# A Fourier-mixing and squared-RELU kernel: 89 instead of 82 halved steps, folds and transform placed earlier, the row read on ScalarE's queue

## The chip, the cores and the metric

The kernel runs on one core of a Trainium2 chip. The metric is the device time of one execution in microseconds. Three executions of the kernel before the change gave 614.35, 612.79 and 614.75 us, with a median of 614.35 us. Below, PE is TensorE, ACT is ScalarE, DVE is VectorE, POOL is GpSimd and SP is SyncE.

## The reference

The input x has shape 8 x 3008 x 256. The real part of its two-dimensional Fourier transform (over the sequence and over the 256 features) is taken as 24064 tokens of 256 features, and goes through a feed-forward layer with a squared RELU.

```python
X = np.fft.fft(x, axis=1)
X = np.fft.fft(X, axis=2)
attn = X.real.astype(np.float32).reshape(8 * 3008, 256)

h = np.maximum(attn @ w_in, 0.0)          # w_in: 256 x 2048
out = (h * h @ w_out).astype(np.float32)  # w_out: 2048 x 256
```

## The kernel before

**Symmetry.** The transform of real data is symmetric, so the kernel works with 12040 *columns* (8 batches, with 4 x 376 + 1 each) that stand for a frequency and its mirror. For each it computes two rows of 128: zc (the cosine part over the features) and zs (the sine part). The feature transform is folded into the first weights. gh holds three forms of them: gh[:, 0] for zc, gh[:, 1] for zs, and gh[:, 2], which is -2 times gh[:, 1] but for the first row, which is zero (the scale is made in `turn2`). With p = gh0 zc and q = gh1 zs, the hidden value of a column is p + q and that of its mirror is p - q, but for row 0 of zs (the d = 128 feature), which enters both with the same sign.

**Windows.** The columns are cut into 25 windows, here called blocks 0 to 24: the first six are 240, 512, 376, 376, 512 and 448 wide, the others 512 and the last 360. The loop `for w in range(NW)` goes over them.

**Steps.** A block has NST = 8 steps s, one for each pair of 128 rows of the 2048 hidden ones. Between the matmuls of a step, `others(s)` issues all other work, in this order: the jobs of at[s], a share of the second layer (`ffn2_steps`, L620) of the block before, post[s], and a share of the transform of the units that begin in the next block (`z_steps`, L482). The order on every queue is the order in which the code issues the instructions.

A *plain* step (`pq`, `turn`, `square`) runs four matmuls for p + q (L731, L732), ScalarE's RELU (L741), then, after `others`, two more matmuls that turn the sum in PSUM into p - q (L737), and a second RELU. The square of each half is made by VectorE (L746), or for the first half by ScalarE (L744) if the step stands in `by_act`.

A *halved* step (`half_q`, `half_p`, `row_sum`, `halves`) runs two matmuls for q (L756), which ScalarE copies out times -2 into sn (L764), and after `others` two more that add p to q in PSUM (L770), which ScalarE copies into hd (L772). VectorE does the rest for a group of one to three neighbouring steps: two rows per step, eb times wv, put back what the sign change took from row 0 (L780); sn becomes sn + rows (L784); the mirror's value is hd + sn (L795); a maximum with 0 (L796); and the square into h2 (L797). L795 to L797 are issued by `halves` in the step after the group's last.

PLAN says which steps of a block are halved and in what groups, and which squares of plain steps ScalarE makes. `plan(w)` picks one of three; blocks 0, 1, 2 and 4 have none. The h2 of a block is read in the next block: step 0 there multiplies the first 128 columns with all 16 chunks of h2, chunks 0 to 7 first, then 8 to 15. Columns of the mirrored half come from step 4 on.

**The row.** Row 0 of zs is needed on all partitions as eb. `row_spread(w)` writes it to DRAM (zr, L581, ScalarE's queue), and reads it back spread over 128 partitions (eb, L583, SP's queue, which also carries the stores of out, L600).

**Folds.** Each batch is folded before its transform, on VectorE, by `fold_jobs(i)`: even fold of the features (L352 to L354), its cosine sum (L362), odd fold (L357, which also issues the load of the next x on POOL), sine sum (L365), differences (L372), a small column (L377 to L379), even sums (L383, written to DRAM on POOL), and their read back. The first two are the *first folds* of a batch; `first_at` places them in steps 0 and 5 of a block. `fold_at` places the rest, two blocks ahead of the batch's columns, at steps 0 and 4 to 7. `late_at` places the four late folds (L408, L419) at steps 3 to 6.

**The transform.** A unit is a batch's odd or even frequencies (16 units). Its plus part is copied by ScalarE into the zc and zs of the windows it falls into (L491); its mirrored columns come from VectorE (L498, `minus`). `lo` and `hi` say over which steps a block spreads it, from lo to hi - 1.

```python
lo, hi = 0, NST - 1
...
if s >= lo:
    for j in spread(zl, s - lo, hi - lo) if s < hi else []:
        j()
```

Of the buffers, PSUM has two for a step's sums, hd has two, sn has two, h2 has two.

By these rules blocks 10, 13, 16 and 19 have fold work and a transform, 11, 14, 17 and 20 have five halved steps and a transform, and 12, 15 and 18 have late folds and the next batch's first folds.

Of the kernel before, what the change touches and what calls it, by code (L numbers as in the profile page):

```python
# [12 lines left out]
ALU = mybir.AluOpType  # L13

HS = 32.0
P = 128
# [12 lines left out]
def kernel(  # L29
# [14 lines left out]
    nc = tc.nc  # L44
# [12 lines left out]
    FIRST = [240, 512, 376, 376, 512, 448]  # L57
    R23 = float(2.0 ** 23)

    PLAN = {0: (((1, 2), (3, 4), (5,)), (0, 6, 7)), 1: (((1, 2), (3, 4)), (0, 5, 6)), 2: (((1, 2), (3,)), (0, 5, 6))}  # L60

    RQ = (1, 3, 5, 0, 2, 4)

# [12 lines left out]
    g = 0  # L76
# [4 lines left out]
    NW = len(wins)  # L81
# [9 lines left out]
    g = 0  # L91
# [91 lines left out]
    def small(shape, name):  # L183
        return const.tile(shape, F32, name=name)
# [271 lines left out]
    def zwin(w):  # L456
        if w not in zc:
            zc[w] = zp.tile([P, WN], F16, name="zc", tag="zc")
            zs[w] = zp.tile([P, WN], F16, name="zs", tag="zs")
        return zc[w], zs[w]  # L460
# [67 lines left out]
    def run(*jobs):  # L528
        for j in jobs:
            j()  # L530
# [34 lines left out]
    wv = small([P, NFC], "wv")  # L565
# [6 lines left out]
        nc.vector.tensor_scalar(out=wv, in0=pv[:, 0:NFC], scalar1=2.0, scalar2=None, op0=ALU.mult)  # L572

    eb = {}

    def row_spread(w):

        wn = wins[w][1]
        t = eb[w] = tmp.tile([P, WN], F16, name="eb", tag="kf")
        zr = drp.tile([1, WN], F16, name="zr", tag="zr")  # L580
        nc.scalar.dma_start(out=zr[0:1, 0:wn], in_=zwin(w)[1][0:1, 0:wn])  # L581
        src = zr[0:1, 0:wn]
        nc.sync.dma_start(out=t[:, 0:wn], in_=bass.AP(tensor=src.tensor, offset=src.offset, ap=[[0, P], [1, wn]]))  # L583

    def store(osb, p0, g0, m, minus, eng=nc.sync):

# [71 lines left out]
    fold_at, late_at = {}, {}  # L658
# [3 lines left out]
    NST = NFC // 2  # L662

    first_at = {}
    for w, i in fold_at.items():
        first_at[w - 1] = i

    def plan(w):

        if w < 3 or w == 4:  # L670
            return (), ()
        return PLAN[min(2, 2 * (w in fold_at) + (w in first_at) + (w in late_at))]

    def halved(w):

        return plan(w)[0]
# [4 lines left out]
    for w in range(NW):  # L681
        g0, wn = wins[w]
        h2 = h2p.tile([P, NFC, 2 * WN], F16, name="h2", tag="h2")
        zcw, zsw = zwin(w)

        lo, hi = 0, NST - 1
        at = [[] for _ in range(NST)]
        post = [[] for _ in range(NST)]
        if w == 0:
# [1 line left out]
        elif w == 1:  # L691
# [3 lines left out]
            lo, hi = 6, 7  # L695
# [11 lines left out]
        elif w == win_of(col_of[1, 1]) - 1:  # L707
            for st in range(4):
                at[st] = folds[1]["late"][st : st + 1]
            lo = 4  # L710
# [16 lines left out]
        def pq(s):  # L727
            ph = phs[s] = ps_h.tile([P, 2, 512], F32, name="ph", tag="psh")
            for a in range(2):
                f0 = (2 * s + a) * P  # L730
                nc.tensor.matmul(ph[:, a, 0:wn], gh[:, 0, f0 : f0 + P], zcw[:, 0:wn], start=True, stop=False)  # L731
                nc.tensor.matmul(ph[:, a, 0:wn], gh[:, 1, f0 : f0 + P], zsw[:, 0:wn], start=False, stop=True)  # L732

        def turn(s):
            for a in range(2):
                f0 = (2 * s + a) * P
                nc.tensor.matmul(phs[s][:, a, 0:wn], gh[:, 2, f0 : f0 + P], zsw[:, 0:wn], start=False, stop=True, skip_group_check=True)  # L737

        def square(s, sg):
            h1 = h1p.tile([P, 2, 512], F16, name="h1", tag="h1")  # L740
            nc.scalar.activation(h1[:, :, 0:wn], phs[s][:, :, 0:wn], AF.Relu)  # L741
            hv = rev_dim(h1[:, :, 0:wn], 2) if sg else h1[:, :, 0:wn]
            if sg == 0 and s in by_act:
                nc.scalar.activation(h2[:, 2 * s : 2 * s + 2, 0:wn], hv, AF.Square)  # L744
                return []
            return [lambda: nc.vector.tensor_tensor(h2[:, 2 * s : 2 * s + 2, sg * wn : (sg + 1) * wn], hv, hv, op=ALU.mult)]  # L746

        two = {s: g for g in halved(w) for s in g}
        by_act = plan(w)[1]
        sns, hds = {}, {}  # L750

        def half_q(s):
            ph = phs[s] = ps_h.tile([P, 2, 512], F32, name="ph", tag="psh")
            for a in range(2):
                f0 = (2 * s + a) * P
                nc.tensor.matmul(ph[:, a, 0:wn], gh[:, 1, f0 : f0 + P], zsw[:, 0:wn], start=True, stop=True)  # L756
            g = two[s]
            if s == g[0]:
                i = ROT[0] % 2
                ROT[0] += 1  # L760
                sns[g] = const.tile([P, 2 * len(g), WN], F16, name=f"sn{i}", tag=f"w16_{i}")
                hds[g] = tmp.tile([P, 2 * len(g), 2 * WN], F16, name="hd", tag="tt")
            i = 2 * g.index(s)
            nc.scalar.activation(sns[g][:, i : i + 2, 0:wn], ph[:, :, 0:wn], AF.Copy, bias=0.0, scale=-2.0)  # L764

        def half_p(s):
            ph, g = phs[s], two[s]
            for a in range(2):
                f0 = (2 * s + a) * P
                nc.tensor.matmul(ph[:, a, 0:wn], gh[:, 0, f0 : f0 + P], zcw[:, 0:wn], start=False, stop=True, skip_group_check=True)  # L770
            i = 2 * g.index(s)
            nc.scalar.activation(hds[g][:, i : i + 2, 0:wn], ph[:, :, 0:wn], AF.Copy, bias=0.0, scale=1.0)  # L772

        def row_sum(s):

            g = two[s]
            sn, hd = sns[g][:, :, 0:wn], hds[g][:, :, wn : 2 * wn]

            def row(a):
                nc.vector.tensor_scalar(out=hd[:, 2 * g.index(s) + a, :], in0=eb[w][:, 0:wn], scalar1=wv[:, 2 * s + a : 2 * s + a + 1], scalar2=None, op0=ALU.mult)  # L780

            jobs = [lambda: row(0), lambda: row(1)]
            if s == g[-1]:
                jobs.append(lambda: nc.vector.tensor_tensor(sn, sn, hd, op=ALU.add))  # L784
            return jobs

        def halves(s):

            if s not in two or s != two[s][-1]:
                return []  # L790
            g = two[s]
            sn, hd = sns[g], hds[g]
            hv = hd[:, :, 0 : 2 * wn]
            return [
                lambda: nc.vector.tensor_tensor(rev_dim(hd[:, :, wn : 2 * wn], 2), hd[:, :, 0:wn], sn[:, :, 0:wn], op=ALU.add),  # L795
                lambda: nc.vector.tensor_scalar(out=hv, in0=hv, scalar1=0.0, scalar2=None, op0=ALU.max),  # L796
                lambda: nc.vector.tensor_tensor(h2[:, 2 * g[0] : 2 * g[-1] + 2, 0 : 2 * wn], hv, hv, op=ALU.mult),  # L797
            ]

        def others(s):  # L800
            for j in at[s]:
                j()
            for j in spread(f2, s, NST):
                j()
            for j in post[s]:
                j()
            if s == lo:
                zl[:] = [j for zu, part, h in zj for j in zu(part, h)]
            if s >= lo:
                for j in spread(zl, s - lo, hi - lo) if s < hi else []:  # L810
                    j()
# [3 lines left out]
        for s0 in range(0, NST, ng):  # L815
            ss = range(s0, s0 + ng)
            left = halves(s0 - 1)
            if s0 in two:
                half_q(s0)
                rows = row_sum(s0)  # L820
                run(*(left[0:1] + rows[0:1] + left[1:2] + rows[1:2] + left[2:3] + rows[2:3]))
                others(s0)
                half_p(s0)
                continue
            for s in ss:
                pq(s)
            for s in ss:
                run(*(left[0:2] + square(s, 0) + left[2:3]))
            others(s0)
            for s in ss:  # L830
                turn(s)
            for s in ss:
                run(*square(s, 1))
            if s0 == hi - 1 and ng == 1 and w + 1 < NW and halved(w + 1):
                row_spread(w + 1)
            for s in ss[1:]:
                others(s)
            if s0 < hi <= s0 + ng - 1 and w + 1 < NW and halved(w + 1):
                row_spread(w + 1)
        old = (w, h2)  # L840
    for j in ffn2_steps(*old, tail=True):
        j()
# [30 lines left out]
```

## Time and profile before

| | |
|---|---|
| median of three runs | 614.35 us |
| the profiled execution | 614.29 us |
| its span in the profile | 612.4 us |
| granted TensorE clock | 0.995 |
| PE busy | 586.7 us, 4400 matmuls |
| PE weight loads busy | 423.4 us |
| ACT busy | 518.0 us |
| DVE busy | 486.7 us |
| POOL busy | 83.3 us |
| DMA | 50.20 MB |

All times within the profile count from the start of the span. A line of a timeline gives the start and the length of an instruction in us, the engine, the line of the code, the operation, what it writes and reads with the shapes, and in brackets how long the engine stood idle before it and what ended that. On PE and on VectorE instructions overlap a little, so that the time from one start to the next says more about what one costs than its own length does.

The blocks can be found in the trace by PE's first-layer matmuls. Block 12 begins at 287.57, block 13 at 311.03, block 14 at 335.64, block 15 at 359.72 and block 16 at 383.18 us. From block 11 to block 20 the pattern repeats every three blocks, some 72.15 us.

### The profile page before, as it was taken

How to read it: one execution, taken by the hardware profiler on the slowest of the kernel's cores; microseconds unless marked ns; L12 is line 12 of the kernel's file. 1: busy time of each engine (PE TensorE's matmuls, PEld its weight loads, DVE VectorE, ACT ScalarE, POOL GpSimd, SP SyncE). 2: the span in 40 equal slices, each digit the busy share in tenths (PEclk: the TensorE clock that was granted, in tenths of full speed). 3: DMA queues.
4: the chain of work that ended last, by engine and by line, in shares of the span. 5: the costliest groups of instructions: out<-in, count | busy, mean ns of one | idle time of the engine just before them, and what ended most of it. 6: DMA issues, size and time to landing. Idle time of an engine off the chain costs nothing.

```text
span 612.4 us, 11453 instructions
## 1 busy us (share of the span) xinstructions
PE 586.7 (96%) x4400; PEld 423.4 (69%) x4400; DVE 486.7 (79%) x742; ACT 518.0 (85%) x673; POOL 83.3 (14%) x125
## 2 busy tenths in 40 slices
PE   5799998999899999999999999999999999998996
PEld 2456876777677777777777767777677777776686
DVE  7787669776978978869979699778997697796980
ACT  7687788888889889889899898898988998988872
POOL 5324110012001021020022200411010200100000
PEclk9899999999999999999999999999999999999999
DMA  8927120173113531632145311543111411111112
GB/s 143 200 80 144 57 81 27 53 155 105 43 52 73 133 115 47 142 115 58 39 100 130 91 55 42 110 121 84 50 36 61 122 44 52 48 50 47 50 56 67
DMA packets 39591, 50.20 MB, mean 82 GB/s; under 512 B 4572, under 2 KB 33393, under 8 KB 39537
## 3 DMA queue, kind: packets, MB, share of 16 engines
q0 software_dynamic: 9344, 22.14, 17.9%
q1 hardware_dynamic: 29923, 27.11, 15.0%
q8 instruction: 34, 0.56, 0.4%
q10 hardware_dynamic: 270, 0.23, 0.1%
q14 instruction: 20, 0.16, 0.1%
HBM read 36.29 MB, written 27.86 MB: 105 GB/s over the span
## 4 chain that ended last, share of the span: by engine, by line
PE 63%; DVE 16%; ACT 8%; issue 6%; DMA 5%; POOL 1%; SPq 0%; ACTq 0%; DVEq 0%; POOLq 0%
PE po L620 37%; PE ph L737 5%; PE ph L770 5%; PE ph L731 4%; PE ph L732 4%; PE ph L756 4%; ACT h L741 4%; DVE h L797 3%; DVE hd L795 3%; DVE hd L796 3%; DMA out_dram<-osb 3%; PE pz L482 3%; ACT hd L772 2%; DMA w<-in_moe_w_in_dram 1%; DVE sn L784 1%
## 5 line engine op out<-in xcount | busy, mean ns | idle before, releaser
L620 PE MATMUL po<-wout,h 128*128 128x256 f16 (+1 forms) x3024 | 362.5, 273 | 1.1 <-DVE h L797 1.0
L620 PEld LDWEIGHTS <-h 128*128 128x128 f16 (+1 forms) x3024 | 296.3, 98 | 73.5 <-DVE h L797 2.5
L741 ACT ACTIVATE h<-ph 128x1024 f16<-128x1024 f32 (+4 forms) x236 | 217.3, 962 | 31.2 <-PE ph L737 16.7
L746 DVE TENSOR_TENSOR h<-h 128x1024 f16<-128x1024 f16 (+4 forms) x173 | 108.0, 641 | 52.0 <-ACT h L741 49.8
L772 ACT ACTIVATE hd<-ph 128x1024 f16<-128x1024 f32 (+3 forms) x82 | 81.4, 993 | 19.2 <-PE ph L770 17.4
L797 DVE TENSOR_TENSOR h<-hd 128x4096 f16<-128x4096 f16 (+7 forms) x50 | 91.7, 1835 | 0.4
L731 PE MATMUL ph<-zc,gh 128*128 128x512 f16 (+4 forms) x236 | 85.2, 363 | 3.8 <-DVE zc L498 3.0
L732 PE MATMUL ph<-zs,gh 128*128 128x512 f16 (+4 forms) x236 | 85.1, 363 | 0.4 <-ACT zs L491 0.4
L764 ACT ACTIVATE sn<-ph 128x1024 f16<-128x1024 f32 (+3 forms) x82 | 81.2, 990 | 0.0
L784 DVE TENSOR_TENSOR sn<-sn,hd 128x2048 f16<-128x2048 f16 (+7 forms) x50 | 49.9, 997 | 31.3 <-ACT sn L764 30.0
L737 PE MATMUL ph<-zs,gh 128*128 128x512 f16 (+4 forms) x236 | 65.5, 363 | 5.1 <-ACT h L741 3.6
L635 ACT ACTIVATE osb<-po 128x512 f32<-128x512 f32 (+3 forms) x95 | 54.6, 578 | 17.1 <-PE po L620 15.1
L744 ACT ACTIVATE h<-h 128x1024 f16<-128x1024 f16 (+3 forms) x63 | 64.8, 1029 | 2.0
L795 DVE TENSOR_TENSOR hd<-hd,sn 128x2048 f16<-128x2048 f16 (+7 forms) x50 | 49.9, 998 | 14.3 <-ACT hd L772 12.1
L780 DVE TENSOR_SCALAR hd<-eb,wv 128x512 f16<-128x512 f16 (+3 forms) x164 | 51.5, 352 | 5.8 <-DMA eb<-zr 5.8
L796 DVE TENSOR_SCALAR hd<-hd 128x4096 f16<-128x4096 f16 (+7 forms) x50 | 49.9, 997 | 0.7
L770 PE MATMUL ph<-zc,gh 128*128 128x512 f16 (+3 forms) x164 | 47.3, 370 | 1.0 <-ACT sn L764 0.8
L756 PE MATMUL ph<-zs,gh 128*128 128x512 f16 (+3 forms) x164 | 47.4, 370 | 0.0
L731 PEld LDWEIGHTS <-gh 128*128 128x128 f16 x236 | 23.0, 97 | 27.5 <-DVE zc L498 3.8
L732 PEld LDWEIGHTS <-gh 128*128 128x128 f16 x236 | 23.0, 98 | 25.1 <-issue 2.0
L425 POOL COPY xt<-xt 128x2 f16<-128x2 f16 x16 | 7.0, 469 | 206.7 <-DVE xt L408 206.7
L737 PEld LDWEIGHTS <-gh 128*128 128x128 f16 x236 | 22.3, 97 | 12.9 <-issue 8.2
(121 smaller groups left out, 381.1 us busy)
## 6 DMA issues: line engine op xcount, KB each, us to landing
out_dram<-osb SPq DMA_DIRECT2D x77, 128.0 KB
xo<-in_x_dram POOLq DMA_DIRECT2D x7, 768.0 KB
scr<-ev POOLq DMA_DIRECT2D x8, 390.0 KB, 3.3
eb<-zr SPq DMA_DIRECT2D x18, 128.0 KB
rb<-scr POOLq DMA_DIRECT2D x16, 130.0 KB
out_dram<-osb SPq DMA_DIRECT2D x12, 94.0 KB
w<-in_moe_w_in_dram POOLq DMA_DIRECT2D x2, 512.0 KB
wout<-in_moe_w_out_dram POOLq DMA_DIRECT2D x1, 1024.0 KB
```

The source lines that it names most:

```text
L620: nc.tensor.matmul(po[0:m, j * D : (j + 1) * D], h2[:, fc, q : q + m], wout16[:, fc, :], start=(fc == 0), stop=(fc == NFC - 1))
L731: nc.tensor.matmul(ph[:, a, 0:wn], gh[:, 0, f0 : f0 + P], zcw[:, 0:wn], start=True, stop=False)
L732: nc.tensor.matmul(ph[:, a, 0:wn], gh[:, 1, f0 : f0 + P], zsw[:, 0:wn], start=False, stop=True)
L737: nc.tensor.matmul(phs[s][:, a, 0:wn], gh[:, 2, f0 : f0 + P], zsw[:, 0:wn], start=False, stop=True, skip_group_check=True)
L741: nc.scalar.activation(h1[:, :, 0:wn], phs[s][:, :, 0:wn], AF.Relu)
L746: return [lambda: nc.vector.tensor_tensor(h2[:, 2 * s : 2 * s + 2, sg * wn : (sg + 1) * wn], hv, hv, op=ALU.mult)]
L756: nc.tensor.matmul(ph[:, a, 0:wn], gh[:, 1, f0 : f0 + P], zsw[:, 0:wn], start=True, stop=True)
L764: nc.scalar.activation(sns[g][:, i : i + 2, 0:wn], ph[:, :, 0:wn], AF.Copy, bias=0.0, scale=-2.0)
L770: nc.tensor.matmul(ph[:, a, 0:wn], gh[:, 0, f0 : f0 + P], zcw[:, 0:wn], start=False, stop=True, skip_group_check=True)
L772: nc.scalar.activation(hds[g][:, i : i + 2, 0:wn], ph[:, :, 0:wn], AF.Copy, bias=0.0, scale=1.0)
L795: lambda: nc.vector.tensor_tensor(rev_dim(hd[:, :, wn : 2 * wn], 2), hd[:, :, 0:wn], sn[:, :, 0:wn], op=ALU.add),
L797: lambda: nc.vector.tensor_tensor(h2[:, 2 * g[0] : 2 * g[-1] + 2, 0 : 2 * wn], hv, hv, op=ALU.mult),
```

## The change

The plan gets new groups. A block with five halved steps keeps (1,2), (3,4), (5). Blocks with fold work or late folds get four halved steps in the groups (1,2) and (4,5), with ScalarE squaring in steps 0, 3 and 6 (before they had three, (1,2) and (3), with squares in 0, 5 and 6; blocks 6 and 21 had four, (1,2) and (3,4)). Block 7 goes from four, (1,2) and (3,4), to five. Blocks 3, 5 and 9 get (1,2) and (4). So there are 89 halved steps in place of 82: block 3 has two fewer, blocks 7, 8, 10, 12, 13, 15, 16, 18 and 19 have one more.

The first folds of batches 5, 6 and 7 move from blocks 12, 15 and 18 to 11, 14 and 17. In block 3 and from block 5 on, the transform is spread over steps 0 to 5 instead of 0 to 6, and the row's write (zr) comes at the end of step 5 instead of 6. The read back (eb) goes out on ScalarE's queue after the block's last step. The rows of a group are all made at its last step instead of two in each.

```diff
-    PLAN = {0: (((1, 2), (3, 4), (5,)), (0, 6, 7)), 1: (((1, 2), (3, 4)), (0, 5, 6)), 2: (((1, 2), (3,)), (0, 5, 6))}
+    PLAN = {
+        "5": (((1, 2), (3, 4), (5,)), (0, 6, 7)),
+        "4": (((1, 2), (4, 5)), (0, 3, 6)),
+        "3": (((1, 2), (4,)), (0, 5, 6)),
+    }
...
-        nc.sync.dma_start(out=t[:, 0:wn], in_=bass.AP(tensor=src.tensor, offset=src.offset, ap=[[0, P], [1, wn]]))
+        row_back.append(lambda: nc.scalar.dma_start(out=t[:, 0:wn], in_=bass.AP(tensor=src.tensor, offset=src.offset, ap=[[0, P], [1, wn]])))
...
     for w, i in fold_at.items():
-        first_at[w - 1] = i
+        free = [v for v in range(w - 1, 6, -1) if v not in late_at and all(not v <= u < w for u in fold_at)]
+        first_at[free[0] if free else w - 1] = i
...
-        return PLAN[min(2, 2 * (w in fold_at) + (w in first_at) + (w in late_at))]
+        if w < 6 or w in first_at and w in late_at:
+            return PLAN["3"]
+        return PLAN["4" if w in fold_at or w in late_at else "5"]
...
-        lo, hi = 0, NST - 1
+        lo, hi = 0, NST - 2 if w == 3 or w > 4 else NST - 1
...
             def row(a):
-                nc.vector.tensor_scalar(out=hd[:, 2 * g.index(s) + a, :], in0=eb[w][:, 0:wn], scalar1=wv[:, 2 * s + a : 2 * s + a + 1], scalar2=None, op0=ALU.mult)
-
-            jobs = [lambda: row(0), lambda: row(1)]
-            if s == g[-1]:
-                jobs.append(lambda: nc.vector.tensor_tensor(sn, sn, hd, op=ALU.add))
-            return jobs
+                nc.vector.tensor_scalar(out=hd[:, a, :], in0=eb[w][:, 0:wn], scalar1=wv[:, 2 * g[0] + a : 2 * g[0] + a + 1], scalar2=None, op0=ALU.mult)
+
+            if s < g[-1]:
+                return []
+            return [lambda a=a: row(a) for a in range(2 * len(g))] + [lambda: nc.vector.tensor_tensor(sn, sn, hd, op=ALU.add)]
...
                 rows = row_sum(s0)
-                run(*(left[0:1] + rows[0:1] + left[1:2] + rows[1:2] + left[2:3] + rows[2:3]))
+                run(*(left[0:1] + rows[0:1] + left[1:2] + rows[1:-1] + left[2:3] + rows[-1:]))
                 others(s0)
                 half_p(s0)
+                if s0 == hi - 1 and w + 1 < NW and halved(w + 1):
+                    row_spread(w + 1)
                 continue
...
+        while row_back:
+            row_back.pop()()
         old = (w, h2)
```

More of the change, by code (lines that the diff above doesn't have):

```diff
@@ L574 @@
     eb = {}
+    row_back = []
     def row_spread(w):
```

## The prediction

> **What bounds the kernel now.** A *block* is one of the 25 windows of columns (at most 512 wide), a *step* one of its eight pairs of 128 rows of the hidden layer. I read the page's busy times first, then the busy time by block over one period of three, then VectorE's timeline in such a block, then the waits.
>
> ```profile
> PE 586.7 (96%) x4400; PEld 423.4 (69%) x4400; DVE 486.7 (79%) x742; ACT 518.0 (85%) x673; POOL 83.3 (14%) x125
> ```
>
> ```profile
> 311.03:335.64 24.61, 24.50 (x193) 17.98 (x192) 20.44 (x28) 22.46 (x30) 5.29 (x6) 1.00 0.55 117
> 335.64:359.72 24.08, 24.08 (x179) 17.41 (x178) 17.81 (x26) 21.36 (x29) 3.13 (x4) 1.00 0.29 88
> 359.72:383.18 23.46, 23.39 (x171) 16.54 (x170) 22.10 (x35) 20.87 (x25) 1.48 (x4) 1.00 0.16 49
> ```
>
> The lines are blocks 13 (with a fold), 14 (five halved steps) and 15 (late fold): length, then busy PE, PEld, DVE, ACT. PE is full in each, and within a block a 512-column matmul follows the last after 0.216 us and a 256-column one after 0.109 us. PE's work decides while nobody makes it wait. But VectorE has 22.10 of 23.46 us in block 15, and what counts for it is when its last result of a block arrives:
>
> ```profile
> 345.95 1.23 DVE L795 TENSOR_TENSOR hd<-hd,sn 128x2048 f16<-128x2048 f16 x1 [0.67 <-ACT hd L772]
> 347.09 0.35 DVE L780 TENSOR_SCALAR hd<-eb,wv 128x512 f16<-128x512 f16 x1
> 347.36 1.22 DVE L796 TENSOR_SCALAR hd<-hd 128x4096 f16<-128x4096 f16 x1
> ...
> 348.75 2.29 DVE L797 TENSOR_TENSOR h<-hd 128x4096 f16<-128x4096 f16 x1
> 350.95 0.61 DVE L780 TENSOR_SCALAR hd<-eb,wv 128x512 f16<-128x512 f16 x2
> 351.67 1.23 DVE L784 TENSOR_TENSOR sn<-sn,hd 128x2048 f16<-128x2048 f16 x1
> 353.00 1.23 DVE L795 TENSOR_TENSOR hd<-hd,sn 128x2048 f16<-128x2048 f16 x1
> ...
> 360.58 1.23 DVE L797 TENSOR_TENSOR h<-hd 128x2048 f16<-128x2048 f16 x1
> 361.72 0.60 DVE L498 SCALAR_TENSOR_TENSOR zc<-es,pz 128x195 f16<-128x195 f32 x2
> ```
>
> ```profile
> 361.86 0.55 PEld L620 LDWEIGHTS <-h 128*128 128x128 f16 x6 [0.30 <-DVE h L797]
> ```
>
> From 345.95, when ScalarE has copied step 2's sums (L772), VectorE has no gap until 361.81, 15.85 us: a **tail** that is its own bound. Its last halved result (step 5) ends 2.09 us after block 15 began at 359.72. The second product of that block reads it 1.95 us in (0.87 for step 0's first four matmuls, eight of 0.109, two more), and so the weight load waits 0.30 and PE loses 0.19. VectorE idles before the tail, in steps 1 and 2, where the results that it needs don't exist yet. So each us that the change puts into the tail of block 14 is a us of PE.
>
> Block 13's tail is also gapless, from 321.04:
>
> ```profile
> 334.21 0.54 DVE L498 SCALAR_TENSOR_TENSOR zc<-es,pz 128x376 f16<-128x376 f32 x1
> 334.67 1.29 DVE L746 TENSOR_TENSOR h<-h 128x1024 f16<-128x1024 f16 x2
> ```
>
> Its last urgent result is the second of these squares (step 7), done at 335.96, 0.32 after block 14's start; PE needs it 2.39 us in (0.87 and fourteen of 0.109). Here 2.1 us are free.
>
> ```profile
> PE ph L737 <- ACT h L741: 3.6, 6, 1.4
> PE ph L731 <- DVE zc L498: 3.0, 2, 1.7
> ```
>
> These waits (total, times, longest) are the transform's: at the ends of blocks 3, 6 and 22 PE or ScalarE waits for the mirrored half (L498) queued behind VectorE's tail. Spacing of PE's matmuls beyond their streaming shows 1.9, 1.4 and 2.9 us there.
>
> **The change, part by part.** Durations are of the profiled execution, 614.29 us (span 612.4); the median is 614.35, so the sum carries over unchanged. "Slot" is start to next start.
>
> *Halved steps.* Each saves two of six first-layer matmuls, 2 x 0.216 = 0.43 us. By the plan there are 82 before and 89 after: one more in blocks 7, 8, 10, 12, 13, 15, 16, 18, 19, two fewer in block 3 (376 columns, 4 x 0.157 = 0.63). PE alone: -9 x 0.43 + 0.63 = -3.2 us. ScalarE evicts twice either way. VectorE pays: slots are 0.27 a row, 1.14 the sum, 1.14 + 1.13 + 2.20 difference, maximum and square for a pair, so 3.3 per halved step against 0.6 or 1.2 for a plain one's squares.
>
> *Rows together at a group's last step.* The rows that stood between difference, maximum and square no longer do. A row starts 0.09 before the end of what precedes it, a dependent operation 0.03 to 0.10 after it (351.67 + 1.23 to 353.00), so each uncovered dependency costs 0.12 to 0.19; I take 0.13, 0.26 a pair. The Trainium skill ("VectorE: DVE Perf Modes", the section on the DRAIN that can't be avoided) says that the next operation doesn't start until the pipe is empty and that chaining without semaphores gains nothing; by it this term would be 0 and the sum about 2 us lower, but the trace's row at 347.09 starts before 347.18 and disagrees.
>
> *Block 14's kind (11, 14, 17), first folds a block sooner.* Ahead of the step-5 square come: the fold's cosine sum at step 5 (slot 0.88, from the equal fold sum at 329.91), the zc mirror (0.52, now 361.72 to 362.24 behind the square, a step sooner ahead of it), 0.26 of uncovered dependencies, and 0.13 since the transform's twelve 0.157 us matmuls lie in six steps instead of seven and step 3 begins later. Together 1.79; nothing leaves this tail. +1.79 x 3 = +5.4. The first even fold (2.0) falls at step 0 into VectorE's idle time. It needs x a block sooner: in block 13 the last gather of x goes out on POOL at 325.68 and such a gather lands in 8.1 us (median), near 334, while VectorE gets to the fold near 339; without that cover the fold and all behind it on VectorE would wait.
>
> *Block 13's kind (10, 13, 16, 19), groups (1,2),(4,5).* Out of the tail go two rows 0.53, step 3's sum 0.60, its triple 2.48, three plain squares 1.8, together 5.4; in come four rows and a dependency 1.19, a sum 1.14, a triple 4.73, a square 0.60, dependencies 0.26, together 7.9. The end moves from 335.96 to 338.5, the next block from 335.64 to 334.93 (0.43, and a 0.28 wait for ScalarE behind two SQUAREs in a row, now apart). 3.6 after its start against 2.39: a stall of 1.3. Net -0.43 - 0.28 + 1.3 = +0.6, x 4 = +2.4.
>
> *Block 15's kind (12, 15, 18), first fold gone.* The tail is 15.7 us from 9.5 us into a block of 22.7 (3 x 2.62 and the rest at 3.05 before): it ends 2.5 late against 2.39, stall 0.2; a 0.22 wait for ScalarE goes. Net -0.45 x 3 = -1.35.
>
> *Single blocks.* 7: one step, one group and 1.2 of mirrors more before the last square (ends 194.6, block 8 from 190.0): -0.43 - 0.31 + 2.6 = +1.9. 8: a fold block without transform, -0.43 + 0.8 = +0.4. 20: like 14 without the cosine sum, +0.9. 23: +0.2. 9, 21: none. 3: +0.63 - 1.9 = -1.3. 6: -1.4 + 0.5 = -0.9. 22: -2.9 + 1.3 = -1.6, for a step sooner the mirrors come before the last triple.
>
> *The row's read on ScalarE.* The eb issue takes 0.35 on SP (L583). At the block's end it stands ahead of the next block's first RELU, 18 times, 6.3 us of ScalarE in all. Its write zr is two steps old by then; at 356.89 it was issued and at 358.01 the read went out, so 1.1 us, and ScalarE won't wait. I take 0, because PE stalls for VectorE at most of these joints while ScalarE, at 89 to 91% of a block, catches up; without this cover it is 0 to 0.35 each, up to +6.3. On SP the stores get free of the wait for zr, which costs nobody now: ScalarE's copies into osb wait for PE alone. VectorE waits for eb three times, 5.8 us in all, in idle time: 0, at most -1.
>
> Sum: 5.4 + 2.4 - 1.35 + 1.9 + 0.4 + 0.9 + 0.2 - 1.3 - 0.9 - 1.6 = **+6.0**, so 620.3 us.
>
> **Rivals.** *VectorE's tail has room (faster).* If the tail's last square comes less than 1.95 us into the next block, PE's streaming decides: -3.2, and the gaps go (1.9, 1.4, 2.9, four of 0.28, four of 0.22: -8.2), so 603. For it: VectorE is busy 79% overall. Against: that share holds the idle steps 1 and 2; the tail shows no gap, and the work is inserted into it. 0.13.
>
> *The stalls are half as long (same).* A tail 0.8 us shorter per block over some ten blocks is -8 at most; at -6 nothing is left, about 614. My tails are good to some 0.3 us. 0.12.
>
> *ScalarE takes the bound (slower still).* With 85% it is the busiest after PE, and every step costs it two evictions as before; then only its new 6.3 us show: 620.6 with no other effect, 626 on top of the sum. Against: its waits are short and on PE. The Trainium skill ("Perfetto Trace Analysis", on identifying the most-contended engine) judges TensorE by weight-load share, not by matmul share; by it, with 69%, ScalarE would be the engine to watch. The spacing of 0.216 and 0.109 us in the trace speaks against it. 0.10.
>
> The forecast has 0.65. A difference below 0.3% (1.8 us) can't be told from none. Faster: the first rival and a sliver, 0.14; same 0.12; slower 0.74. The range takes in the second rival and most of the third, 612 to 625.
>
> **What would show it.** After: PE waiting for L797's successor at the starts of blocks 12, 15, 18 some 2 us, at those of 11, 14, 17, 20 some 1.3 us; no gap at the ends of 3, 6 and 22; blocks 14 and 13 with their following stall near 25.9 and 25.2 us, 15 near 23. VectorE's tail gapless and 17.6 us in block 14. It is wrong if VectorE shows gaps in that tail, or if PE waits for ScalarE's first RELU instead.

## The result and the profile after

Four executions of the changed kernel took 621.57 us in the median (619.85 to 623.12), against 614.55 for four of the kernel before on the same chip: the ratio is 1.0118, with a 95% interval of 1.0084 to 1.0152. So the change makes the kernel 7.0 us slower; the forecast was 620.3. In the traces PE's first block begins at 21.3 to 24.7 us, whatever the kernel, and this alone shifts single runs by up to 3 us, so the text also counts from there to the end of the span: 588.95 us before and 596.33 after, 7.4 more.

The busy line of the page after:

```profile
PE 584.0 (94%) x4386; PEld 421.0 (68%) x4386; DVE 503.7 (81%) x742; ACT 519.1 (84%) x673; POOL 85.3 (14%) x125
```

PE has less work (584.0 us against 586.7), as 89 halved steps want it, and VectorE has 17.0 us more. Yet PE's share of the span fell. Where its time went shows in the busy times by block; the columns are as before, and the lines are blocks 13, 14 and 15 of the changed kernel:

```profile
312.11:336.33 24.22, 24.18 (x191) 17.78 (x190) 21.12 (x28) 22.12 (x30) 4.44 (x6) 1.00 0.57 115
336.33:361.61 25.28, 24.26 (x180) 17.33 (x179) 22.50 (x32) 21.94 (x29) 3.69 (x5) 1.00 0.28 85
361.61:386.46 24.85, 23.01 (x169) 16.34 (x168) 21.02 (x29) 20.84 (x25) 0.42 (x2) 1.00 0.16 48
```

Before, PE was busy for all but 0 to 0.11 us of each. Now blocks 14 and 15 hold 1.02 and 1.84 us in which it is idle, and together the three are 74.35 us long in place of 72.15. VectorE's timeline of block 14:

```profile
347.99 1.23 DVE L802 TENSOR_TENSOR hd<-hd,sn 128x2048 f16<-128x2048 f16 x1 [0.67 <-ACT hd L780]
349.25 1.23 DVE L803 TENSOR_SCALAR hd<-hd 128x4096 f16<-128x4096 f16 x1
350.51 2.29 DVE L804 TENSOR_TENSOR h<-hd 128x4096 f16<-128x4096 f16 x1
352.72 1.14 DVE L788 TENSOR_SCALAR hd<-eb,wv 128x512 f16<-128x512 f16 x4
353.96 1.23 DVE L792 TENSOR_TENSOR sn<-sn,hd 128x2048 f16<-128x2048 f16 x1
355.11 0.61 DVE L502 SCALAR_TENSOR_TENSOR zs<-es,pz 128x195 f16<-128x195 f32 x2
...
361.22 0.97 DVE L366 TENSOR_TENSOR ab<-fe 128x1560 f16<-128x1560 f16 x1
362.11 0.61 DVE L502 SCALAR_TENSOR_TENSOR zc<-es,pz 128x195 f16<-128x195 f32 x2
...
364.08 1.22 DVE L804 TENSOR_TENSOR h<-hd 128x2048 f16<-128x2048 f16 x1
```

The tail runs without a gap from 347.99 to 365.30, 17.31 us; it was 15.85, and 17.6 was forecast. The cosine sum (L366) and the zc mirror (L502) stand ahead of the last triple, where the forecast put them. Block 15 began at 361.61, so its last square is 3.69 us late. PE's weight loads at the start of blocks 14 and 15:

```profile
339.90 0.11 PEld L625 LDWEIGHTS <-h 128*128 128x128 f16 x2 [1.29 <-DVE h L754]
...
365.35 0.55 PEld L625 LDWEIGHTS <-h 128*128 128x128 f16 x6 [1.91 <-DVE h L804]
```

The first waits for the plain square of block 13's step 7 (L754), the second for the last halved square of block 14 (L804; this wait was 0.30 us before the change). In the waits of the whole changed kernel (total, times, longest), these two head those of PE's weight loads:

```profile
PEld L625 <- DVE h L804: 11.7, 7, 2.3
ACT h L749 <- DVE h L754: 11.8, 12, 1.9
PEld L625 <- DVE h L754: 6.5, 6, 1.3
PE ph L778 <- ACT sn L772: 2.0, 8, 0.4
```

The second and the last were not in the forecast, and come up again below.

### The profile page after: what moved, and what is told of

Read it like the earlier page. It is cut to its first block, busy times and chain, and to the rows that moved or that the text cites. A ratio compares the mean times of both kernels' runs of the same rounds, so it can differ in the third digit from the quotient of the medians.

```text
span 618.1 us, 11384 instructions
## 1 busy us (share of the span) xinstructions
PE 584.0 (94%) x4386; PEld 421.0 (68%) x4386; DVE 503.7 (81%) x742; ACT 519.1 (84%) x673; POOL 85.3 (14%) x125
## 4 chain that ended last, share of the span: by engine, by line
PE 45%; DVE 29%; issue 10%; ACT 10%; DMA 4%; POOL 1%; ACTq 0%; DVEq 0%; SPq 0%; POOLq 0%
PE po L625 27%; DVE h L804 7%; DVE hd L803 5%; DVE hd L802 5%; ACT h L749 4%; PE ph L745 4%; PE ph L778 3%; PE ph L764 3%; PE ph L739 3%; PE ph L740 3%; DMA out_dram<-osb 3%; DVE hd L788 2%; DVE h L754 2%; ACT sn L772 2%; DVE sn L792 2%
## 5 line engine op out<-in xcount | busy, mean ns | idle before, releaser
L749 ACT ACTIVATE h<-ph 128x1024 f16<-128x1024 f32 (+4 forms) x222 | 204.8, 951 | 34.0 <-PE ph L745 13.7
L754 DVE TENSOR_TENSOR h<-h 128x1024 f16<-128x1024 f16 (+4 forms) x159 | 97.5, 632 | 38.9 <-ACT h L749 36.9
L804 DVE TENSOR_TENSOR h<-hd 128x4096 f16<-128x4096 f16 (+7 forms) x50 | 100.0, 1999 | 1.3
L780 ACT ACTIVATE hd<-ph 128x1024 f16<-128x1024 f32 (+3 forms) x89 | 89.1, 1001 | 12.3 <-PE ph L778 11.8
L772 ACT ACTIVATE sn<-ph 128x1024 f16<-128x1024 f32 (+3 forms) x89 | 88.8, 998 | 0.0
L739 PE MATMUL ph<-zc,gh 128*128 128x512 f16 (+4 forms) x222 | 79.6, 361 | 1.1 <-ACT h L749 0.8
L740 PE MATMUL ph<-zs,gh 128*128 128x512 f16 (+4 forms) x222 | 79.6, 361 | 0.4 <-ACT zs L495 0.4
L640 ACT ACTIVATE osb<-po 128x512 f32<-128x512 f32 (+3 forms) x95 | 54.6, 578 | 21.3 <-PE po L625 17.2
L745 PE MATMUL ph<-zs,gh 128*128 128x512 f16 (+4 forms) x222 | 61.0, 361 | 2.2 <-ACT h L749 1.2
L778 PE MATMUL ph<-zc,gh 128*128 128x512 f16 (+3 forms) x178 | 51.7, 371 | 2.0 <-ACT sn L772 2.0
L764 PE MATMUL ph<-zs,gh 128*128 128x512 f16 (+3 forms) x178 | 51.7, 372 | 0.0
L740 PEld LDWEIGHTS <-gh 128*128 128x128 f16 x222 | 21.6, 98 | 23.7 <-issue 2.5
L739 PEld LDWEIGHTS <-gh 128*128 128x128 f16 x222 | 21.6, 97 | 22.4 <-DVE zc L502 0.5
L764 PEld LDWEIGHTS <-gh 128*128 128x128 f16 x178 | 17.3, 97 | 20.0
```

## The experiments

Two theories stood against each other. The *tail theory* is the forecast's: PE waits for VectorE's last urgent square. The *ScalarE theory* says that ScalarE, with the row's read on its queue, is what holds PE up. Each ratio is to runs of the kernel before on the same chip. The last column is the time from the start of PE's first block to the end of the span, in the one trace of each kernel (588.95 us before the change); "in the traces" below means differences of this column.

| kernel | median us | ratio to before | 95% interval | trace, from PE's first block, us |
|---|---|---|---|---|
| the change | 621.57 | 1.0118 | 1.0084 to 1.0152 | 596.33 |
| fold_in_idle | 612.82 | 0.9988 | 0.9972 to 1.0003 | 588.52 |
| first_folds_back | 620.93 | 1.0124 | 1.0092 to 1.0156 | 596.55 |
| row_read_on_sp | 619.95 | 1.0105 | 1.0077 to 1.0132 | 595.83 |
| only_early_transform | 609.35 | 0.9930 | 0.9908 to 0.9952 | 585.60 |
| late_mirrors | 618.34 | 1.0080 | 1.0052 to 1.0108 | 594.54 |
| old_groups_three_early | 608.37 | 0.9915 | 0.9890 to 0.9941 | 584.38 |
| all_89_idle | 610.94 | 0.9950 | 0.9931 to 0.9969 | 586.65 |
| idle_less_squares | 605.33 | 0.9860 | 0.9835 to 0.9884 | 581.82 |
| old_groups_four_last | 608.02 | 0.9907 | 0.9884 to 0.9930 | 583.46 |

### The fold work out of the tails (fold_in_idle)

```diff
-            at = [fj[2:3], [], [], [], fj[3:4], fj[4:5], fj[6:7], fj[7:8]]
+            at = [fj[2:3], fj[3:4], fj[4:5], [], [], [], fj[6:7], fj[7:8]]
...
-            at[5] = at[5] + fj[1:2]
+            at[1] = at[1] + fj[1:2]
```

> The changed kernel with the fold work taken out of VectorE's tails: the first cosine sum at step 1 instead of 5, the sine sum at 1 instead of 4, the differences at 2 instead of 5. Nothing else moves, no engine gets more or less work. Tail theory (PE stands still at a block's start because VectorE's last urgent square comes late): the 1.8 us stalls after blocks 11, 14 and 17 and the 2.2 after block 7 shrink by the cosine sum's 0.88 each, the 1.2 after blocks 10, 13, 16 and 19 vanish (1.76 leaves their tails) and so does the 0.5 after block 8: 3.5 + 4.7 + 0.5 = 8.7 us, so 8.7 us faster than the changed kernel, about 613, level with the one before. ScalarE theory (its queue with 18 more reads is what PE waits for): no change, 621.

Measured: 612.82 us, 8.75 less than the changed kernel by the medians and 7.8 less in the traces. No instruction was added, removed or given to another engine; three per batch stand some steps sooner in VectorE's order. Its timeline has the cosine sum in step 1 of block 14 (which begins at 333.66), ahead of the tail, and PE's weight load at the start of block 15 waits about half as long:

```profile
339.14 0.97 DVE L366 TENSOR_TENSOR ab<-fe 128x1560 f16<-128x1560 f16 x1
...
359.32 1.23 DVE L804 TENSOR_TENSOR h<-hd 128x2048 f16<-128x2048 f16 x1
360.46 0.68 DVE L754 TENSOR_TENSOR h<-h 128x1024 f16<-128x1024 f16 x1
```

```profile
360.60 0.55 PEld L625 LDWEIGHTS <-h 128*128 128x128 f16 x6 [1.02 <-DVE h L804]
```

The matmuls' spacing gives 0.92 us of stall there in place of 1.80, and none after blocks 10, 13, 16 and 19. The stalls that the tail theory named shrink by 8.8 us in all, as foretold (8.7); the traces differ by less because block 17 loses 1.3 us at another place, which is taken up below. The ScalarE theory, which foresaw no change, falls for these stalls.

### The first folds back (first_folds_back)

```diff
-        first_at[free[0] if free else w - 1] = i
+        first_at[w - 1] = i
...
-        if w < 6 or w in first_at and w in late_at:
+        if w < 6 or w == 9:
```

> The changed kernel with the first folds of batches 5, 6 and 7 put back into blocks 12, 15 and 18; 89 halved steps and all else stay. Tail theory: the cosine sum of 0.88 us leaves the tails of 11, 14 and 17 (stall 1.8 to 0.9) and enters those of 12, 15 and 18 (0.2 to 1.1), so the sum stays within 1 us of the changed kernel, and the trace shows the stalls in the other place. ScalarE theory: no change in the sum nor in the places. If the earlier first folds themselves were the loss: 3 us faster.

Measured: 620.93 us, 0.6 less by the medians, with intervals that overlap, and 0.2 more in the traces. The stall moves as foretold. At the start of block 12 and of block 13:

```profile
290.54 0.55 PEld L625 LDWEIGHTS <-h 128*128 128x128 f16 x6 [1.02 <-DVE h L804]
```

```profile
314.73 0.11 PEld L625 LDWEIGHTS <-h 128*128 128x128 f16 x2 [0.82 <-DVE h L754]
```

The first was 1.9 in the changed kernel, the second wasn't there. Blocks 12, 15 and 18 are 0.88 us shorter each, and the blocks behind them 0.88 longer: the cosine sum costs its 0.88 us in whichever tail it stands, and placing the fold a block sooner lost nothing by itself.

### The row's read on SP (row_read_on_sp)

```diff
-        row_back.append(lambda: nc.scalar.dma_start(out=t[:, 0:wn], in_=...))
+        nc.sync.dma_start(out=t[:, 0:wn], in_=...)
```

> The changed kernel with the row's read back (eb) issued on SP's queue right behind its write again; all else stays. Tail theory: within 1 us of the changed kernel, for the read's 0.35 us on ScalarE lies where PE waits for VectorE. ScalarE theory: 18 x 0.35 = 6.3 us faster, about 615.

Measured: 619.95 us, 1.6 less than the changed kernel, and 0.5 less in the traces; the intervals overlap, so the size is open, but 6.3 is out of reach. The joint after block 14 is as before the edit:

```profile
364.65 0.55 PEld L625 LDWEIGHTS <-h 128*128 128x128 f16 x6 [1.91 <-DVE h L804]
```

Block 5 is 0.4 us shorter: there ScalarE's first RELU had stood behind the read, and no stall covered it. Block 13 is 0.3 shorter for a cause that the trace doesn't name, for there the read had gone out 1.2 us before the RELU that came late. Block 20 is 0.85 longer: on SP the read for block 19 went out only 3.0 us into that block, VectorE's rows waited for it, and the tail of block 19 ended later:

```profile
468.35 1.14 DVE L788 TENSOR_SCALAR hd<-eb,wv 128x512 f16<-128x512 f16 x4 [3.07 <-DMA eb<-zr]
```

### The early transform alone (only_early_transform)

```diff
 (against the kernel before)
-        lo, hi = 0, NST - 1
+        lo, hi = 0, NST - 2 if w == 3 or w > 4 else NST - 1
...
                 half_p(s0)
+                if s0 == hi - 1 and w + 1 < NW and halved(w + 1):
+                    row_spread(w + 1)
                 continue
```

> The kernel before with the transform and the row's write a step sooner, in block 3 and from block 5 on, and nothing else of the change: 82 halved steps in the old groups, eb on SP. Tail theory: the waits for the mirrored columns at the ends of blocks 3, 6 and 22 go (1.9 + 1.4 + 2.9 = 6.2), and where five halved steps and a transform meet (11, 14, 17, 20) the zc mirror now stands ahead of the last square, +0.65 each = +2.6: 3.6 us faster than the kernel before, about 611. ScalarE theory: it has the same work, so only the waits that ScalarE itself had for the mirrors, in 6 and 22, some 3 us, go.

Measured: 609.35 us, 4.9 less than the kernel before (by the medians of this table's runs, 614.20) and 3.4 less in the traces, for the 3.6 expected. Blocks 3, 6 and 22 became 1.7 (0.35 of it back in block 4), 1.3 and 3.0 us shorter, and the stalls after 11, 14, 17 and 20 grew from 0.19 to 0.67:

```profile
361.85 0.55 PEld L620 LDWEIGHTS <-h 128*128 128x128 f16 x6 [0.78 <-DVE h L797]
```

So this part of the change gains where PE waits for the mirrors and loses where they get ahead of the last square.

### The mirrors back behind the last square (late_mirrors)

```diff
-        lo, hi = 0, NST - 2 if w == 3 or w > 4 else NST - 1
+        lo, hi = 0, NST - 2 if w in (3, 6, 22) else NST - 1
```

> The changed kernel with the transform over seven steps again (and the row's write at step 6), but for blocks 3, 6 and 22, which keep six; all else stays. Tail theory: the zc mirror (0.52) goes back behind the last square and step 3 comes 0.13 sooner, so the stalls after blocks 11, 14, 17 shrink from 1.80 to 1.15 and after 20 from 0.91 to 0.26, after block 7 (0.6 of zc mirrors and more) from 2.16 to about 1.0; the 1.18 after 10, 13, 16, 19 stay, for there both mirrors still stand ahead of step 7's square. In all 3.8 us faster than the changed kernel, about 617.8. If the mirrors didn't count in the tail: no change.

Measured: 618.34 us, 3.2 less by the medians. In the traces it is 1.8 less, and 1.1 of that is only the last stores, which landed sooner after ScalarE's last copy. The stalls after 11, 14 and 17 went from 1.80 to 1.31, after 20 from 0.91 to 0.43, after 7 from 2.16 to 1.60. Those after 10, 13, 16 and 19 fell too, from 1.18 to 0.72, which I had not foreseen: their blocks became some 0.3 to 0.4 us longer, with a wait of 0.42 us for ScalarE in step 4, so that VectorE had this time more. So the mirrors do count in the tail, but the sum of 3.8 is not borne out: the stalls lost 4.4 us in all, and new waits for ScalarE took most of it back, the four of 0.42 us and, where ScalarE stood behind the row's read, 1.0 in block 22 and 0.6 in block 17. That the medians come near 3.8 is in part luck.

### Versions that use both findings

*old_groups_three_early* makes the same edit to only_early_transform.

> The kernel before with the transform and the row's write a step sooner in blocks 3, 6 and 22 alone: 82 halved steps in the old groups, eb on SP. Tail theory: the gains of the early transform at these three blocks' ends (some 5.5 us) without the stalls of 0.67 that it brought after 11, 14, 17 and 20: 607 to 608.5, faster than every kernel so far. If the early transform gains everywhere else too: slower than 609.4.

Measured: 608.37 us, within the range expected. The stalls after 11, 14, 17 and 20 are back at 0.18 us.

*all_89_idle* is fold_in_idle with the early transform in three blocks, the late folds moved, and the row's read on SP:

```diff
-                at[st + 3] = at[st + 3] + folds[late_at[w]]["late"][st : st + 1]
+                to = st + 3 if w < 12 else 1 + st // 2
+                at[to] = at[to] + folds[late_at[w]]["late"][st : st + 1]
```

> All 89 halved steps with the tails emptied: the cosine sum at step 1, sine sum 1, differences 2, from block 12 on the late folds at steps 1 and 2 (instead of 3 to 6), the early transform in blocks 3, 6 and 22 alone, the row's read on SP behind its write. Tail theory: of the stalls that were left with the folds moved (0.92 after 11, 14, 17, 1.09 after 20, 1.28 after 7) some 0.25 each stay, so 4 us less than that kernel's 612.8, and up to 1.6 from the read: 607 to 609, and with the stalls gone the seven steps at last count. If ScalarE bounds by then: 611 or more, with waits on RELU and copies in the place of those on squares.

Measured: 610.94 us, so 2 to 4 more than I expected. The stalls after 11, 14 and 17 did shrink, to 0.43, but blocks 10, 13, 16 and 19 got a wait of 0.42 in step 4 by the matmuls' spacing, and a stall behind them of 0.30 (0.65 behind block 19). These are the lines of PE and then of ScalarE in block 13:

```profile
325.63 0.59 PE L779 MATMUL ph<-zc,gh 128*128 128x512 f16 x2 [0.25 <-ACT sn L773]
```

```profile
321.83 1.06 ACT L753 ACTIVATE h<-h 128x1024 f16<-128x1024 f16 x1
322.79 0.58 ACT L640 ACTIVATE osb<-po 128x512 f32<-128x512 f32 x1
323.27 0.48 ACT L491 ACTIVATE es<-pz 128x377 f32<-128x377 f32 x1
323.64 1.03 ACT L750 ACTIVATE h<-ph 128x1024 f16<-128x1024 f32 x1
324.54 1.04 ACT L773 ACTIVATE sn<-ph 128x1024 f16<-128x1024 f32 x1
```

ScalarE squares for step 3, copies out two other results, does step 3's second RELU, and reaches step 4's copy sn late; PE's second pair (L779) waits for it. Here ScalarE does hold up PE, as the second theory had it, but by the plan's squares and not by the row's read, which is on SP here; the next version tests the square.

*idle_less_squares* takes that square away from step 3:

```diff
-        "4": (((1, 2), (4, 5)), (0, 3, 6)),
+        "4": (((1, 2), (4, 5)), (0, 6, 7)),
...
+        if w in (22, 23):
+            return ((1, 2), (3, 4)), (0, 5, 6)
```

> As the last, and two more: in blocks with the groups (1,2) and (4,5) ScalarE squares in steps 0, 6 and 7 instead of 0, 3 and 6, and blocks 22 and 23 have four halved steps, (1,2) and (3,4), with squares in 0, 5 and 6. Tail theory: the 0.37 us that PE waits for ScalarE's copy in step 4 (behind its square of step 3) goes in five blocks, and the waits of 1.07 and 1.40 after blocks 22 and 23 go for 2 x 0.43 of PE: 3 to 3.5 us less than the last, about 604.5. ScalarE theory: two squares in a row at a block's end hold up the next RELU, 0.2 to 0.4 each in some ten blocks, so no gain.

Measured: 605.33 us, 1.4% faster than the kernel before by the medians (7.1 us in the traces, 1.2%) and the fastest of all. The waits in step 4 fell to 0.11 us in blocks 10, 13, 16 and 19, and went in 8, 12, 15, 18 and 21. Of the ScalarE theory's price 0.20 us came at the start of blocks 11, 14 and 17, where PE waits for the first RELU behind step 7's square. The lines by block for 13, 14 and 15:

```profile
306.01:329.95 23.94, 23.94 (x192) 17.70 (x191) 21.35 (x26) 21.70 (x30) 4.35 (x4) 1.00 0.56 115
329.95:354.23 24.28, 24.24 (x180) 17.41 (x178) 22.10 (x33) 22.12 (x30) 3.67 (x5) 1.00 0.33 91
354.23:377.42 23.19, 22.93 (x170) 16.34 (x169) 21.50 (x30) 20.59 (x24) 1.59 (x4) 1.00 0.16 49
```

PE is busy for 71.11 of 71.41 us again, with VectorE's work as large as in the changed kernel (64.95 us against 64.65).

*old_groups_four_last* asks what the halved steps are worth; against old_groups_three_early, it has four of them in blocks 22 and 23:

```diff
+        if w in (22, 23):
+            return PLAN[1]
```

> The kernel with the old groups and the three early transforms, and with four halved steps, (1,2) and (3,4), in blocks 22 and 23 too: 80 halved steps, against the 87 of the fastest kernel so far. Tail theory: the stalls of 1.03 and 1.14 after these blocks go for 2 x 0.43 of PE: 1.3 us faster than 608.4, about 607.1. The fastest kernel's seven more halved steps (3.0 us of PE) would then be worth 1.8 us once the folds lie in VectorE's idle time. If the stalls weren't the last squares': 0.9 slower, 609.2, and the seven steps would be worth all of 3.9.

Measured: 608.02 us. The medians differ by 0.35, less than they spread; in the trace the stretch from block 22 to the end is 0.9 us shorter, and the two stalls are gone. Of the two readings the trace bears out the first; the medians alone leave it open. So the seven more halved steps of idle_less_squares, with its other edits, are worth 2.7 us by the medians and 1.6 in the traces, where 1.8 was expected and they save 3.0 of PE; the size lies open between these.

## Why the prediction was right

The path was the one forecast: the tail got longer by what was put into it, the block shorter by what PE saved, and PE waited for the difference. Positions are not compared from the span's start, for PE's first block begins at 23.41 us before and at 21.74 after. Of these 1.7 us, 0.5 is the first weights' DMA, for which PE waits until 16.09 in one and 15.57 in the other. The rest goes with the clock granted from 16 to 20 us, 0.62 in one and 1.00 in the other: the first two matmuls behind that wait took 1.03 us in one and 0.60 in the other. Counted from the first block, the change costs 7.4 us. A block is taken here with the stall behind it instead of the one at its start:

| blocks | forecast us | measured us |
|---|---|---|
| 11, 14, 17 | +5.4 | +5.0 |
| 10, 13, 16, 19 | +2.4 | +2.3 |
| 12, 15, 18 | -1.35 | -0.7 |
| 7 | +1.9 | +1.55 |
| 8 | +0.4 | +0.45 |
| 20, 23 | +1.1 | +1.0 |
| 22 | -1.6 | -1.8 |
| 6 | -0.9 | -0.9 |
| 3 and 4 | -1.3 | -0.6 |
| 5, 21, 24 | 0 | +1.1 |
| sum | +6.0 | +7.4 |

**Halved steps.** PE's busy time shrank by 2.7 us on the page, for 3.2 in the sum.

**Block 14's kind.** The last square is 3.69 us late, against 3.88 by the sum (2.09 and 1.79). The stall went from 0.19 to 1.80. The terms hold one by one; what the sum lacked is that the zs mirror now stands between a sum (353.96) and the difference that reads it, and covers 0.18 us: from the sum's start to the next start it is 1.15 us (353.96 to 355.11) where it was 1.33 (351.67 to 353.00).

**Block 13's kind.** The two squares that it ends on, the second of them step 7's, are in the trace after

```profile
338.56 1.28 DVE L754 TENSOR_TENSOR h<-h 128x1024 f16<-128x1024 f16 x2
```

and end at 339.84, 3.51 us after block 14's start at 336.33; 3.6 was forecast. The stall is 1.18 for 1.3, and the 0.28 wait for ScalarE is gone.

**Block 15's kind.** Here a term was left out. Step 3's square on ScalarE makes step 4's copy late, 0.37 us in each of blocks 8, 12, 15, 18 and 21; idle_less_squares, without that square, has none of these waits. I had followed ScalarE through the joints and not through the new by_act.

**Blocks 3 to 5, and 24.** I let all of the 1.9 us at block 3's end go. 0.37 and 0.42 of new waits took their place. Block 5 lost 0.38 behind the row's read on ScalarE's queue; row_read_on_sp has it back. Block 24's 0.6 is the landing of the last stores, 5.0 us after ScalarE's last copy instead of 4.4, and it varies from kernel to kernel (3.9 to 5.0).

**The row's read.** "ScalarE won't wait" was right for most blocks and not for all, and what it costs is at most the 1.6 us that row_read_on_sp gained. The 6.3 us counted 18 reads; there are 21, three of them for narrower blocks. The forecast also took the time from the row's write to its read from a single row, 1.1 us; over all blocks before the change it was 1.1 to 5.3.

PE's stalls as the cover were only a part of the reason. In fold_in_idle the joints after blocks 10, 13 and 19 have no stall, and yet blocks 11, 14 and 20 still take 24.08 us, as before the change. The cover counts where the read itself comes late: in the changed kernel it goes out 2.69 us into block 17, while PE stands still for 1.18 us anyway. In fold_in_idle, which has no stall there, block 17 lost 1.33 us, with ScalarE standing behind the read (issued at 408.38, 2.73 us into the block):

```profile
408.83 1.02 ACT L749 ACTIVATE h<-ph 128x1024 f16<-128x1024 f32 x1 [1.89 <-DVE xo L356]
```

The releaser named there is VectorE's, but the instruction ahead is the read. By the trace's semaphore events (a semaphore is a counter on which an engine waits), the read was not held up by the row's write, which had landed at 404.18. It waited on a semaphore that it shares with a store of out (L605, issued on SP at 399.65), and that store's last part landed at 408.30.

**Rivals.** VectorE's tail had no room: the first rival asked for a last square less than 1.95 us into the block, and it came at 3.69. The stalls were not half as long either. By its number alone the result would also fit the third rival, ScalarE as the bound (620.6 with no other effect). What speaks against it is where PE waits, and that fold_in_idle took these waits away while ScalarE kept all its work. In the versions that follow, ScalarE's squares do hold up PE, by 0.37 to 0.42 us in nine blocks of all_89_idle.

In the Trainium skill, the page "VectorE: DVE Perf Modes", section "The DRAIN you can't avoid", says that the next operation doesn't start until the pipe is empty, but it goes on that one which is not held (kept back until all earlier ones have finished) starts earlier. The prediction quoted the first half alone. The trace after agrees with that: the rows at 352.72, which need nothing of the square ahead of them, start 0.08 us before its end at 352.80, while the maximum at 349.25, which reads the difference of 347.99, starts 0.03 after that one's end. So the page gave no reason to put this term at 0. It came out as taken: difference, maximum and square of a pair now take 4.73 us (347.99 to 352.72), 0.26 more than the 4.47 of their slots before.

The page "Perfetto Trace Analysis" of the Trainium skill, section "Identifying the Most-Contended Engine", measures TensorE's headroom by the share of weight loads together with MFU (the share of the peak arithmetic rate); the prediction named the weight loads alone. In this kernel the share that they leave free is no room: in the fastest kernel they take 72% of the three blocks above (51.46 of 71.41 us), while PE stands still for 0.30 us.

## What to carry to other kernels

Where one engine is nearly full, ask of every other engine not only how busy it is but when its last result of a stage is due, and add up what stands in its queue between the last input and that moment. Work that no one needs in that stretch belongs in the engine's idle time at the stage's start: moving three instructions per batch there was worth 7.8 us in the traces and 8.75 by the medians, and no engine did less work. Once these waits are gone the next engine's order shows (here ScalarE's squares), so a plan of which steps take the short form must be checked against each queue, not against sums of busy time.

## What was not expected of the hardware

Late squares hold up two engines. In the changed kernel ScalarE waits for VectorE's plain squares 12 times, 11.8 us in all (2.1 us in four before), because its next RELU writes one of three buffers of h1 that such a square still reads. That the buffers are the cause is read from the code and not shown: a fourth one wasn't tried. The waits lie mostly inside PE's own stalls.
